# Windowed attention with a mixture of experts: blocks taken by position over all batches, and expert weights as float32 halves on the loads' own queue

## The chip, the cores and the metric

The kernel runs on one core of one Trainium2 chip. The metric is the device time of one execution in microseconds (us). A core has five engines with an instruction stream each: PE (TensorE, matrix products; its weight loads are shown apart as PEld), DVE (VectorE), ACT (ScalarE), POOL (GpSimd) and SP (SyncE, which here only issues DMA transfers). They run side by side and wait for each other by semaphores. Data in main memory comes into SBUF, the on-chip memory of 128 partitions, by DMA; PE writes its results to PSUM.

## The reference

Sliding-window attention with sink keys, then a mixture of four experts over all tokens. The sizes are B, H, S, D = 4, 8, 768, 64; 4 sink keys, a window of 128; 3072 tokens of 512 values, four experts with a hidden layer of 1024.

```python
scores = scale * np.matmul(q, k.transpose(0, 1, 3, 2))
keep = is_sink | in_window            # pos < 4, or 0 <= query - key < 128
scores = np.where(keep, scores, -1000000000.0)
a = softmax(scores)                   # written out in the reference
attn_out = np.matmul(a, v)
x = attn_out.transpose(0, 2, 1, 3).reshape(B * S, H * D)
p = domain_probs / (domain_probs.sum(-1, keepdims=True) + 1e-09)
for e in range(E):
    h = np.maximum(x @ w1[e], 0.0)
    out += p[:, e:e + 1] * (h @ w2[e])
```

Inputs and output are float32. A block of 128 queries needs its own 128 keys, the 128 keys before them, and, from the third block of a batch on, the four sink keys, which then lie outside its window.

## The kernel before

**Units.** The attention is cut into 24 blocks of 128 queries, numbered u = 0 to 23. `divmod(u, NQB)` gives the batch b and the position qb in it: batch 0's six blocks come first, then batch 1's. A block's way is: `load` q, k, v (256 KB each, float32, by SP); `cast` to bfloat16 on POOL; transposes of q and k (`pe_tr` on PE for u < 8, where u = 0 and 1 are transposed in float32 without a cast; `dma_q`, `dma_k` on SP's queue after that); `scores` (L340) into PSUM, against one key block where qb is 0 and two otherwise; `maxima` on DVE (L352: scale, mask and row maximum in one operation per head); `exps` on ACT (L360); transposes of the attention weights (`pe_a` and `a_out` for u < 8, `dma_a` after that); `values` (L420); `sums` and `normalise` on DVE; and a transpose into `xT` (`pe_x` or `dma_x`), which the experts read.

**Sinks.** Blocks with qb >= 2 have scores with the sink keys (`sink_scores`, `sink_minima`, `sink_args`, `sink_exps`). Their part of the result is made in two ways: for u < 8 (UPS) by one more matmul in `values` with a block-diagonal tile `vsd` (L417), and for u >= 8 by `weigh_sinks` on POOL, four products and three sums of 128x512 (L186, L190) that read `vsb`, the batch's sink values spread over all partitions by a transfer of 1 MB. `normalise` adds them (L449).

**Keys.** `kT` holds a batch's transposed keys in six slots, one for each position; two batches are held at a time.

**Experts.** An item is 512 tokens (four blocks) and one expert; the first 512 tokens with expert 0 are four items of 128. `mm1` (L495) makes the hidden layer from `w1[e]` and `xT`, `relu` moves it to SBUF, `mm2` (L521) makes 128 tokens of the output from `w2[e]`, and `collect` adds it, times the token's share, into `out_sb`, which `store` writes out. With `LATE`, the last expert of the first 512 tokens comes after three experts of the next 512. The last group's second layer is `last_group` (L537, L541).

**Weights.** `load_w1` and `load_w2` fetch a whole matrix of an expert (2 MB of float32) by a DMA of POOL's queue that casts to bfloat16 as it goes. The eight are issued after chosen casts of v (`w_after`).

**Order.** Nothing is scheduled on the chip. A planner in the kernel, at build time, keeps a table `nodes` with each step's engines and assumed costs, the steps that it needs, and a due time `want`; it takes the step that can start first, with the earliest due time among equals, and records it. So every engine has one fixed order, and an instruction that waits holds all behind it on its engine. `MOVED` shifts due times by hand. Loads are chained in the order of the list `loads`; the planner's model of the DMA queues (`transfers`, `SHARED`) tells it when data will be there. Until the first `mm2`, `keep_busy` puts matmuls without a use (idle_out, L482) where it sees PE idle.

Of the kernel before, what the change touches and what calls it, by code (L numbers as in the profile page):

```python
# [16 lines left out]
def kernel(  # L17
# [43 lines left out]
    UPS = 8  # L61

    UG = 4

    UF = 2

# [11 lines left out]

    NBS = -(-(UPS - 2) // NQB)
    vs = resid.tile([HS, B, D], FP32, name="vs", tag="vs")  # L80
    vsd = [resid.tile([P, H, D], BF16, name=f"vsd{b}", tag=f"vsd{b}") for b in range(NBS)]
# [3 lines left out]
    dp_nat = consts.tile([NTB, P, E], FP32, name="dp_nat")  # L85
# [7 lines left out]
    skd = [resid.tile([P, NHP, 2, NSINK], BF16, name=f"skd{i}", tag=f"skd{i}") for i in range(2)]  # L93
# [19 lines left out]
    M1 = consts.tile([P, 2, P], FP32, name="M1")  # L113
    M0 = consts.tile([P, P], FP32, name="M0")
    masks = [M0, M1, M2]

# [18 lines left out]
    for m in (M1, M2):  # L135
        nc.vector.memset(m, 0.0)
        own_keys(m[:, 1])
        keys_before(m[:, 0])
    nc.vector.memset(M1[:, 0, 0:NSINK], 0.0)


    bd = consts.tile([HS, H], FP32, name="bd")

    def sink_consts(eng):
        for t in Abuf:
            nc.gpsimd.memset(t[:, 2 * H], 0.0)
        for t in vsd:
            nc.gpsimd.memset(t, 0.0)
# [5 lines left out]
    def sink_heads(eng):  # L154
        nc.vector.reduce_sum(
            out=bd, in_=ident[0:HS, 0:HS].rearrange("p (h r) -> p h r", r=NSINK), axis=AX.X
        )

    def sink_values(eng, b):
        nc.gpsimd.tensor_mul(  # L160
            vsd[b][0:HS], vs[:, b, :][:, None, :].to_broadcast([HS, H, D]),
            bd[:, :, None].to_broadcast([HS, H, D]),
        )

# [3 lines left out]
    def spread_values(eng, b):  # L168
        vsb[b] = at_sb.tile([P, H, NSINK, D], FP32, name="vsb", tag="vsb", bufs=1)
        nc.sync.dma_start(  # L170
            out=vsb[b].rearrange("p h r d -> p h (r d)"),
            in_=v[b, :, 0:NSINK, :].rearrange("h r d -> h (r d)")[None].to_broadcast(
                [P, H, NSINK * D]
            ),
        )

    def sinks_on_pool(u):
        return u >= UPS and u % NQB >= 2

    def weigh_sinks(eng, u):  # L180
# [3 lines left out]
        for r in range(NSINK):  # L184
            t = sv if r == 0 else at_sb.tile([P, H, D], FP32, name="svr", tag="svr", bufs=1)
            nc.gpsimd.tensor_mul(  # L186
                t, vsb[u // NQB][:, :, r], pr[:, :, r : r + 1].to_broadcast([P, H, D])
# [17 lines left out]
    kT = {}  # L205
# [4 lines left out]
    def load(eng, u, what):  # L210
        b, qb = divmod(u, NQB)
# [6 lines left out]
    def cast(eng, u, what):  # L218
        t = raw.pop((what, u))
        if what == "v":  # L220
            vn[u] = resid.tile([P, H, D], BF16, name="vn", tag="vn", bufs=5)
# [15 lines left out]

    def load_sinks(eng):
        for h in range(H):
            nc.sync.dma_start(  # L240
                out=vs[h * NSINK : (h + 1) * NSINK],
                in_=v[:, h, 0:NSINK, :].rearrange("b r d -> r b d"),
            )
# [18 lines left out]
    def keys_of(b):  # L262
        if b not in kT:
            kT[b] = at_sb.tile([P, NHP, NQB, P], BF16, name="kT", tag="kT", bufs=2)
        return kT[b]
# [9 lines left out]
    def dma_k(eng, u):  # L275
        b, qb = divmod(u, NQB)
        nc.sync.dma_start_transpose(
            out=keys_of(b)[:, :, qb],
            in_=nat.pop(("k", u)).rearrange("p h d -> p (h d)"),
        )  # L280
# [13 lines left out]
    def k_out(eng, u):  # L294
        b, qb = divmod(u, NQB)
        copy_on(eng, keys_of(b)[:, :, qb], live.pop(("trk", u)))

    def sink_keys(eng, b):
        for c in range(2):
            r = slice(c * D, (c + 1) * D)  # L300
            copy_on(eng, skd[b % 2][r, :, c], kT[b][r, :, 0, 0:NSINK])
# [735 lines left out]
```

## Time and profile before

Three runs took 395.13, 395.74 and 397.17 us, a median of 395.74. The profiled execution has a span of 395.2 us from its first instruction to its last.

| | busy us | share of the span | instructions |
|---|---|---|---|
| PE | 384.8 | 97% | 2513 |
| PEld | 194.8 | 49% | 2555 |
| DVE | 203.6 | 52% | 672 |
| ACT | 225.6 | 57% | 632 |
| POOL | 147.7 | 37% | 177 |
| span | 395.2 | | |
| TensorE clock granted | 1.000 | | |
| DMA, SP's queue (q1) | 43.09 MB | 51.2% of 16 engines | |
| DMA, POOL's queue (q0) | 8.39 MB | 13.1% of 16 engines | |

How to read it: an engine's busy time is the sum of its instructions. PE's contains matmuls that wait for data within the array and those without a use, so 97% is not yet 97% of useful work. "q1" is the queue that SP fills, "q0" the one that POOL fills; the bytes of q0 are counted after the cast to bfloat16. The share of a DMA queue is the time that its packets took, over 16 DMA engines and the whole span. In the chain of work that ended last, PE has 86% of the span and DMA 11%, most of it in transfers of k and v.

The column of a line group that says "idle before" is the time in which the engine stood idle just ahead of these instructions; behind the arrow is what ended it. In a timeline, the first number is the start, the second how long the entry lasted, and "x4" how many instructions are merged in it.

### The profile page before, as it was taken

Reading aid. Unit: us, or ns where it says so; the run is one execution under the profiler, and the core shown is the slowest. Engines: PE = TensorE matmul, PEld = TensorE weight load, DVE = VectorE, ACT = ScalarE, POOL = GpSimd, SP = SyncE. Lnnn points to the kernel's source line nnn. Section 1 sums busy time; section 2 is a strip of 40 time slices with the busy share of each in tenths; the row PEclk is TensorE's granted clock in tenths of the full one; section 3 lists DMA queues with packets and bytes.
Section 4 is the critical chain, followed back from the end, with each engine's and each line's share of the span. In section 5 each row is a group of like instructions: output and inputs, shape, how many; then the busy total and the mean of one; then the engine's idle time right before and its main releaser. Section 6 shows DMA issues by size and latency. Waiting matters only on the chain.

```text
span 395.2 us, 7309 instructions
## 1 busy us (share of the span) xinstructions
PE 384.8 (97%) x2513; PEld 194.8 (49%) x2555; DVE 203.6 (52%) x672; ACT 225.6 (57%) x632; POOL 147.7 (37%) x177
## 2 busy tenths in 40 slices
PE   8999999999999999999999999999999999999996
PEld 6777555544444444444444444444444444444443
DVE  3996787259364853843866734456455332200233
ACT  5896787666573663764754746466377333354320
POOL 3515050309928561074495740154943800000000
PEclk9999999999999999999999999999999999999999
DMA  8998999918599689986555996762751300200002
GB/s 188 204 203 166 190 200 194 243 40 165 129 148 219 131 194 255 209 195 93 114 111 123 200 226 138 159 140 62 199 120 21 48 13 2 80 28 1 0 2 107
DMA packets 148154, 51.95 MB, mean 131 GB/s; under 512 B 135548, under 2 KB 143100, under 8 KB 148116
## 3 DMA queue, kind: packets, MB, share of 16 engines
q1 hardware_dynamic: 141844, 43.09, 51.2%
q0 software_dynamic: 6272, 8.39, 13.1%
q8 instruction: 20, 0.33, 0.3%
q14 instruction: 18, 0.15, 0.1%
HBM read 38.88 MB, written 6.29 MB: 114 GB/s over the span
## 4 chain that ended last, share of the span: by engine, by line
PE 86%; DMA 11%; issue 1%; POOL 1%; SPq 0%; DVE 0%; POOLq 0%
PE mopsum L521 40%; PE hpsum L495 39%; DMA rawk<-in_k_dram 5%; DMA rawv<-in_v_dram 5%; PE sp L340 3%; PE op L420 2%; DMA rawq<-in_q_dram 1%; PE lpsum L537 0%; PE tra L400 0%; PE trk L286 0%; PE trq L286 0%; PE ss L306 0%; POOL vn L200 0%; PE trx L471 0%; PE idle_out L482 0%
## 5 line engine op out<-in xcount | busy, mean ns | idle before, releaser
L495 PE MATMUL hpsum<-xT,w 128*128 128x512 bf16 (+1 forms) x843 | 182.5, 355 | 1.1
L521 PE MATMUL mopsum<-w,ht 128*128 128x512 bf16 x739 | 175.7, 379 | 1.6 <-issue 0.6
L509 ACT ACTIVATE ht<-hpsum 128x512 bf16<-128x512 f32 x172 | 102.0, 594 | 113.6 <-PE hpsum L495 100.8
L521 PEld LDWEIGHTS <-ht 128*128 128x128 bf16 x760 | 72.9, 98 | 87.7 <-issue 2.7
L495 PEld LDWEIGHTS <-w 128*128 128x128 bf16 x864 | 76.4, 98 | 79.0 <-issue 2.0
L562 DVE SCALAR_TENSOR_TENSOR out_sb<-mopsum,shares,out_sb 128x512 f32<-128x512 f32 x71 | 52.9, 746 | 109.2 <-PE mopsum L521 107.0
L360 ACT ACTIVATE A<-SM,negm 128x256 bf16<-128x256 f32 (+1 forms) x192 | 92.0, 481 | 16.6 <-DVE negm L352 13.6
L352 DVE CUSTOM_DVE_ANT_0 SM<-sp,M,slow 128x256 f32<-128x256 f32 x128 | 54.7, 479 | 8.6 <-PE sp L340 8.4
L190 POOL TENSOR_TENSOR sv<-sv,svr 128x512 f32<-128x512 f32 x36 | 45.6, 1267 | 2.8
L186 POOL TENSOR_TENSOR svr<-vsb,A 128x512 f32<-128x512 f32 x36 | 38.1, 1059 | 1.9
L200 POOL CAST qn<-rawq 128x512 bf16<-128x512 f32 x22 | 13.9, 634 | 62.1 <-DMA rawq<-in_q_dram 60.7
L360 ACT ACTIVATION_READ_ACCUMULATOR A<-SM,negm 128x1 f32 x192 | 36.3, 189 | 0.0
L186 POOL TENSOR_TENSOR sv<-vsb,A 128x512 f32<-128x512 f32 x12 | 13.0, 1082 | 62.5 <-ACT A L374 62.5
L558 ACT ACTIVATE out_sb<-mopsum,shares 128x512 f32<-128x512 f32 x19 | 13.0, 687 | 19.1 <-PE mopsum L521 19.0
L352 DVE CUSTOM_DVE_ANT_0 SM<-sp,M 128x128 f32<-128x128 f32 (+1 forms) x64 | 19.1, 351 | 5.9 <-PE sp L340 5.9
L200 POOL CAST kn<-rawk 128x512 bf16<-128x512 f32 x22 | 13.5, 614 | 19.7 <-DMA rawk<-in_k_dram 19.6
L200 POOL CAST vn<-rawv 128x512 bf16<-128x512 f32 x24 | 15.2, 633 | 12.5 <-DMA rawv<-in_v_dram 12.5
L449 DVE TENSOR_TENSOR both<-op,sv 128x512 f32<-128x512 f32 x12 | 8.3, 688 | 17.4 <-PE op L420 9.6
L340 PE MATMUL sp<-kT,qT 64*128 64x256 bf16 (+1 forms) x192 | 16.8, 271 | 0.0
L352 DVE DVE_READ_ACCUMULATOR2_ANT negm<- 128x1 f32 x192 | 15.9, 83 | 0.0
L420 PEld LDWEIGHTS <-AT 128*128 128x128 bf16 x352 | 13.4, 98 | 4.8 <-issue 0.2
L451 DVE TENSOR_TENSOR xn<-op,rs 128x512 bf16<-128x512 f32 x12 | 8.3, 688 | 14.5 <-PE op L420 14.1
(76 smaller groups left out, 197.5 us busy)
## 6 DMA issues: line engine op xcount, KB each, us to landing
w<-in_moe_w_dram POOLq DMA_DIRECT2D x8, 1024.0 KB, 12.8
rawq<-in_q_dram SPq DMA_DIRECT2D x24, 256.0 KB
rawk<-in_k_dram SPq DMA_DIRECT2D x24, 256.0 KB
rawv<-in_v_dram SPq DMA_DIRECT2D x24, 256.0 KB
out_dram<-out_sb SPq DMA_DIRECT2D x23, 256.0 KB
vsb<-in_v_dram SPq DMA_DIRECT2D x3, 1024.0 KB
AT<-A SPq DMA_TRANSPOSE x32
qT<-qn SPq DMA_TRANSPOSE x16
```

What stands on the lines that cost most here:

```text
L186: nc.gpsimd.tensor_mul(t, vsb[u // NQB][:, :, r], pr[:, :, r : r + 1].to_broadcast([P, H, D]))
L190: nc.gpsimd.tensor_add(sv, sv, t)
L200: nc.gpsimd.tensor_copy(out=out, in_=in_)
L340: nc.tensor.matmul(sp[h % 2][:, h // 2 % 2, lo:2], lhsT=qTb[u % 2][r, h // 2], rhs=kT[b][r, h // 2, qb - 1 + lo : qb + 1], start=True, sto ...
L352: nc.vector.tensor_tensor_reduce(out=SM[:, h][part], in0=live.pop(("sp", u, h))[part], in1=masks[min(qb, 2)], scale=-scale, scalar=live["s ...
L360: nc.scalar.activation(out=Abuf[u % 2][:, 2 * h + lo : 2 * h + 2, :], in_=SM[:, h, lo:2], func=AF.Exp, scale=-1.0, bias=live["negm", u][:, ...
L420: nc.tensor.matmul(op[:, h], lhsT=at[:, 2 * h + i], rhs=vn[u - 1 + i][:, h, :], start=(not sinks and i == lo), stop=(i == 1 and (h == H - ...
L495: nc.tensor.matmul(ps[:, j * n : (j + 1) * n], lhsT=w1[e][:, db, fb * P : (fb + 1) * P], rhs=xT[t0 // 512][:, db, t0 % 512 : t0 % 512 + n] ...
L509: nc.scalar.activation(out=ht, in_=ps, func=AF.Relu)
L521: nc.tensor.matmul(ps, lhsT=hidden(i, fb, sub), rhs=w2[e][:, fb, :], start=(fb == 0), stop=(fb == NFB - 1),)
L558: nc.scalar.activation(out=dst, in_=ps, func=AF.Copy, scale=sc)
L562: nc.vector.scalar_tensor_tensor(out=dst, in0=ps, scalar=sc, in1=dst, op0=ALU.mult, op1=ALU.add)
```

## The change

1. **Order of blocks.** `place(u)` replaces `divmod(u, NQB)`: u runs over the batches first, so that u = 0 to 3 are the first blocks of the four batches, u = 4 to 7 the second ones, and u >= 8 all those with sinks. `tile_of(u)` gives the block's place in the output, which `collect`, `last_group` and `store` now use. A block's neighbour before it is u - 4.
2. **Keys.** Each batch has its own `kT` with two slots, taken in turn by position (`qb % 2`); the mask that fits the swap is `M3`. Three of the masks are now made on POOL, as steps of the plan. Each batch has its own `skd`.
3. **Sinks.** The `vsd` path is gone with its tiles, its loads of `vs` and its matmul. Every block with sinks goes through `weigh_sinks`, and `vsb` is fetched for every such block, 16 times in place of 3.
4. **Weights.** Each matrix comes in two halves of 1 MB float32, by SP's queue, at places in the one list `loads` (`w_at`), into a ring `big` of three buffers that `vsb` shares; POOL or DVE then casts each half in two pieces. `mm1` waits for the half that it reads, `mm2` for both.
5. **Plan.** `LATE` is off: the four experts of the first 512 tokens come first. `starts`, `want_x` and `MOVED` have other numbers, and the DMA model is one queue in order.

```diff
+    NVN = 6
+    NBIG = 3
+    def place(u):
+        qb, b = divmod(u, B)
+        return b, qb
+    def tile_of(u):
+        b, qb = place(u)
+        return b * NQB + qb
...
-    skd = [resid.tile([P, NHP, 2, NSINK], BF16, name=f"skd{i}", tag=f"skd{i}") for i in range(2)]
+    skd = [resid.tile([P, NHP, 2, NSINK], BF16, name=f"skd{b}", tag=f"skd{b}") for b in range(B)]
+    kT = [resid.tile([P, NHP, 2, P], BF16, name=f"kT{b}", tag=f"kT{b}") for b in range(B)]
...
+    def later_mask(eng, m, own):
+        nc.gpsimd.memset(m, 0.0)
+        own_keys(m[:, own])
+        keys_before(m[:, 1 - own])
+        if m is M1:
+            nc.gpsimd.memset(m[:, 0, 0:NSINK], 0.0)
...
+    def big(name):
+        return at_sb.tile([P, 2048], FP32, name=name, tag="big", bufs=NBIG)
+    def spread_values(eng, u):
+        b, qb = place(u)
+        t = big("vsb")
         nc.sync.dma_start(
...
-    def load_w1(eng, e):
-        nc.gpsimd.dma_start(out=w1[e], in_=moe_w1[e].rearrange("(db p) f -> p db f", p=P))
-    def load_w2(eng, e):
-        nc.gpsimd.dma_start(out=w2[e], in_=moe_w2[e].rearrange("(fb p) d -> p fb d", p=P))
+    def half_of(e, layer, i):
+        if layer == 1:
+            fs = slice(i * (F // 2), (i + 1) * (F // 2))
+            return w1[e][:, :, fs], moe_w1[e].rearrange("(db p) f -> p db f", p=P)[:, :, fs]
+        bs = slice(i * (NFB // 2), (i + 1) * (NFB // 2))
+        return w2[e][:, bs], moe_w2[e].rearrange("(fb p) d -> p fb d", p=P)[:, bs]
+    def load_w(eng, e, layer, i):
+        t = big("wraw").rearrange("p (a c) -> p a c", a=4)
+        nc.sync.dma_start(out=t, in_=half_of(e, layer, i)[1])
+        wraw[e, layer, i] = t
+    def cast_w(eng, e, layer, i, j):
+        copy_on(
+            eng, half_of(e, layer, i)[0][:, 2 * j : 2 * j + 2],
+            wraw[e, layer, i][:, 2 * j : 2 * j + 2],
+        )
...
-        sinks = qb >= 2 and not sinks_on_pool(u)
-        if sinks:
-            nc.tensor.matmul(op, lhsT=at[:, 2 * H], rhs=vsd[b], start=True, stop=False)
         for h in range(H):
-            for i in range(lo, 2):
+            for i in blocks:
                 nc.tensor.matmul(
...
+                    op[:, h], lhsT=at[:, 2 * h + i],
+                    rhs=vn[u if i == own else u - B][:, h, :],
+                    start=(i == 0), stop=(i == blocks[-1]),
...
-        if sinks_on_pool(u):
-            both = at_sb.tile([P, H, D], FP32, name="both", tag="both", bufs=1)
-            nc.vector.tensor_add(both, res, live.pop(("sv", u)))
+        if u // B >= 2:
+            both = live.pop(("sv", u))
+            nc.vector.tensor_add(both, res, both)
...
-    LATE = True
+    LATE = False
...
-    w_after = [(2, "v"), (3, "v"), (4, "v"), (5, "v"), (6, "v"), (7, "v"), (10, "v"), (11, "v")]
+    w_at = [(1, 'v'), (2, 'v'), (3, 'k'), (3, 'k'), (3, 'v'), (3, 'v'), (5, 'q'), (5, 'q'), (5, 'k'), (5, 'k'), (5, 'v'), (5, 'v'), (6, 'k'), (7, 'k'), (8, 'k'), (9, 'q')]
+    halves_of_w = [(e, layer, i) for e in range(E) for layer in (1, 2) for i in range(2)]
+    for n, (e, layer, i) in enumerate(halves_of_w):
+        deps = [(("wc",) + halves_of_w[n - NBIG] + (j,), HOP) for j in range(2)] if n >= NBIG else []
+        node(("wl", e, layer, i), {"SP": 0.1}, lambda eng, e=e, l=layer, i=i: load_w(eng, e, l, i),
+             deps, -50.0, dma=2.7)
+        for j in range(2):
+            node(("wc", e, layer, i, j), {"POOL": 1.25, "DVE": 0.65},
+                 lambda eng, e=e, l=layer, i=i, j=j: cast_w(eng, e, l, i, j),
+                 [(("wl", e, layer, i), HOP)], -50.0)
...
+    for u in range(2 * B, NU):
+        if u - NBIG >= 2 * B:
+            deps = [(("sv", u - NBIG), HOP)]
+        else:
+            deps = [(("wc",) + halves_of_w[u - 2 * B - NBIG] + (j,), HOP) for j in range(2)]
+        node(("vsb", u), {"SP": 0.6}, lambda eng, u=u: spread_values(eng, u), deps,
+             nodes["load", u, "v"]["want"] + 0.1, dma=3.0)
...
         for g in range(NG):
+            have_w = [(("wc", e, 1, 2 * g // NG, j), HOP) for j in range(2)]
```

More of the change, by code (lines that the diff above doesn't have):

```diff
@@ L204 @@
     vn = {}
-    kT = {}
     xT = {}
@@ L385, in dma_a @@
         lo = half * H
-        hi = H if half == 0 else 2 * H + (1 if u % NQB >= 2 and not sinks_on_pool(u) else 0)
+        hi = lo + H
         nc.sync.dma_start_transpose(
@@ L832 @@
             d["want"] += MOVED.get(f"i{key[1]}", 0.0) + MOVED.get(key[0], 0.0)
-        elif len(key) > 1 and key[0] not in ("w1", "w2", "load", "sk", "vsd", "vsb"):
-            if key[1] < 9:
+        elif len(key) > 1 and key[0] not in ("wl", "wc", "load", "sk", "vsb", "mask"):
+            if key[1] < 16:
                 for name in (f"u{key[1]}", key[0], f"{key[0]}{key[1]}"):
```

301 lines of the change are left out of this document (124 added, 177 removed), and 4 rows, old and new, of the table MOVED.

## The prediction

> **What bounds the kernel now.** First the stages (busy time of each engine by stretch of the span):
>
> ```profile
> core 0: us, PE busy (x) PEld busy (x) DVE busy (x) ACT busy (x) POOL busy (x), PEclk, DMA share, GB/s
> 0.00:26.50 26.50, 23.33 (x246) 17.68 (x247) 18.75 (x93) 21.14 (x72) 10.60 (x27) 1.00 1.00 197
> 26.50:46.20 19.70, 19.43 (x262) 14.68 (x262) 14.38 (x53) 14.26 (x45) 5.28 (x8) 1.00 1.00 180
> 46.20:80.00 33.80, 32.62 (x261) 17.75 (x265) 20.57 (x79) 25.68 (x78) 8.85 (x14) 1.00 1.06 208
> 80.00:150.00 70.00, 69.47 (x413) 32.44 (x419) 42.26 (x134) 40.91 (x121) 42.69 (x44) 1.00 0.78 150
> ```
>
> From 80 us on PE has 0.5 us idle in 70: the rest of the span is PE's own work and nothing but less PE work shortens it. What can be won lies ahead, where DMA's share is 1.00. Then the timeline of PE there:
>
> ```profile
> 25.12 0.34 PE L482 MATMUL idle_out<-idle_in 128*128 128x128 bf16 x3
> ...
> 26.46 1.06 PE L495 MATMUL hpsum<-xT,w 128*128 128x128 bf16 x16
> ...
> 46.18 3.73 PE L495 MATMUL hpsum<-xT,w 128*128 128x512 bf16 x15
> ...
> 52.58 0.40 PE L286 MATMUL trk<-ident,kn 128*128 128x128 bf16 x4 [0.91 <-POOL kn L200]
> ```
>
> Until 26.46 us PE fills its time with dummies (idle_out); the first expert matmul starts there. The chain and POOL say what it waits for: loads of the attention inputs, while weights use the same DMA engines.
>
> ```profile
> 19.16 14.53 DMA rawv<-in_v_dram
> 34.98 16.78 DMA rawk<-in_k_dram
> ```
>
> ```profile
> 46.20 0.61 POOL L200 CAST qn<-rawq 128x512 bf16<-128x512 f32 x1 [7.62 <-DMA rawq<-in_q_dram]
> 51.91 0.61 POOL L200 CAST kn<-rawk 128x512 bf16<-128x512 f32 x1 [5.09 <-DMA rawk<-in_k_dram]
> ```
>
> A 256 KB load that lands 0.9 us behind its neighbour early on (POOL's casts at 11.11, 12.05 and 12.96 us) takes 14 to 17 us when a weight is under way.
>
> **PE's work, counted.** From the starts of neighbours on PE's timeline: four 512-column L495 matmuls 0.863 us, eight L521 1.73, sixteen 128-column L495 0.90, four float32 transposes 0.88, four bf16 transposes 0.22, a block's scores 0.55 (0.28 with one key block), values 0.46 (0.23), sink scores 0.11, a vsd matmul (L417) 0.21. Over all instructions of before: experts 332, attention 39.5, together 371.4. Of it 11.0 stands ahead of the matmul at 26.46, so PE is 15.5 us behind its work there; e=1's second layer starts at 58.81 with 41.4 ahead of it, 17.4 behind; the last matmul ends at 391.5, 20.1 behind. So 17.4 is lost by 59 us, 2.7 in the 333 us after it, and 3.7 behind the last matmul (span 395.2).
>
> **The change part by part.**
>
> PE work. The four vsd matmuls (L417, 0.9 us) go and 20 of the 116 transposes of L400 (1.1 us: no sink columns, and four early blocks with one key block in place of two); the rest is the same work in another order. After: 369.4, that is -2.0.
>
> Loads. Nothing changes until v of u=1, whose cast starts at 9.61. From there the DMA order is a single line, so landings add up: 0.95 us for each q, k, v load (the POOL casts above) and h for a float32 half of 1 MB. No row shows that transfer. Lower bound: its rows are 2 KB, and packets of 2048 bytes (stores of out_sb) take 84 ns in the packet records, 512 x 84 / 16 = 2.69 us. Upper bound: the old weight queue,
>
> ```profile
> q0 software_dynamic: 6272, 8.39, 13.1%
> ```
>
> 13.1% of 395.2 is 51.8 us for eight matrices of 2 MB float32, 3.24 us for each MB. I take 2.85: the busiest microsecond of the stores starts 187 packets (2.74), and the old queue shared its engines with other packets. Eight tiny vs loads also leave SP (12.90 to 17.88, 5 us in which q of u=4 waited); SP's issue of a load, 0.4 to 1.5 us, stays under the transfer.
>
> Casts of weights: 32 of 128x1024, half of them on POOL and half on DVE in the built order. POOL's 128x512 casts take 0.61, so 1.22 each; DVE's price is bounded by 0.42 (its bf16 PSUM copies, per 512) and 0.69 (its float32 PSUM casts), 0.84 to 1.38. Beside POOL's 1.22 a half is ready 1.2 to 1.4 us after landing; I use 1.2. POOL idles in waits for loads over most of the first 60 us (15.9 busy of 46.2), which hides its 20 us; DVE has 13 us free in the third stage, and about 6 us less to do in u=0 to 3 (32 maxima 0.21 apart, where 8 stood 0.21 and 24 stood 0.35 to 0.41 apart, and no sink work), for casts of 13 to 22 us in all, spread over 80. Without that cover each cast would add its 1.2 us to every gate below. The mask work on POOL (six selects of 0.29, three memsets of 0.2 to 0.5) fits before 9.6, where POOL idles 2.15 and 2.30 us.
>
> Gates. For each wait: landing, plus cast, less the PE work ahead of it, is how far PE is behind.
> - w2 of e=0, second half (4 halves, 5 loads after 9.6): 25.75 + 1.2 - 14.5 = 12.5. The work ahead is the attention of u=0 to 2, the scores and transposes of u=3, and six first-layer groups of 0.90.
> - w1 of e=2, first half (9 halves, 11 loads): 45.7 + 1.2 - 33.4 = 13.5.
> - k of u=6 (12 halves, 14 loads): 57.1 + 0.6 - 44.1 = 13.6.
> - w1 of e=3, first half: 13 halves, 14 loads, 60.0 + 1.2 - 48.7 = 12.5; its second half 11.1.
> - w2 of e=3, second half: near 80, with 74.2 of work ahead: no gate.
>
> The latest is 13.6, and PE does not fall further behind by loads. ACT, nearly full in the first stage (21.14 of 26.5), is not later: 32 exps 0.385 us apart, with its copies and relus, end u=3's attention at 27.2, and its values stand behind one second-layer group (1.73) that starts at the first gate, 27.0.
>
> Later units. All 16 blocks u>=8 weigh their sinks on POOL, 12 before. From
>
> ```profile
> L190 POOL TENSOR_TENSOR sv<-sv,svr 128x512 f32<-128x512 f32 x36 | 45.6, 1267 | 2.8
> L186 POOL TENSOR_TENSOR svr<-vsb,A 128x512 f32<-128x512 f32 x36 | 38.1, 1059 | 1.9
> ```
>
> one costs 3 x 1.27 + 4 x 1.06 = 8.06, with three casts 9.9 us a block. vsb goes from 3 to 16 transfers of 1 MB; one alone (its packets at 233.7 to 238) takes 4.3 us. A block then has on the DMA queue: 4.3, loads 3 x 0.95, five transposes about 3.5 (half a microsecond per 128 KB at 1000 packets a microsecond), a store 0.7: 11.4 us. Between the scores of u=8 and u=15 PE has 84.3 us of work, 12.0 a block; from u=16 it has 14 to 15. SP issues them in line: the wait of vsb for sv of three blocks before holds the transposes behind it, whose casts stand behind the same sv on POOL anyway. So this is covered, by 0.6 us a block; I cost it at nothing and keep both ends: 0, or what the third rival gives.
>
> Sum: 369.4 + 13.6 + 2.7 + 3.7 = 389.4 against a span of 395.2, -5.8. The median of runs stands 0.5 above that span: 389.9, so about 390.
>
> The Trainium skill ("SBUF — State Buffer", Who interferes with whom) speaks against the DVE casts: an SBUF-to-SBUF float32 copy on DVE takes a port pair shared with GpSimd, and one of the two blocks fully. No run here shows it: DVE's copies all read PSUM. By that rule a half's two casts come one after the other, which the second rival prices.
>
> **Rivals.**
> 1. The weight stays as slow as on its old queue (3.24). Then k of u=6 lands at 61.8, 18.3 behind, 394.1 in the span: no change. For it: the same HBM bytes by the same engines. Against: the 256-byte packets that ran beside them then (0.6 to 1.5 thousand per matrix).
> 2. POOL and DVE hold each other up when they cast at once. A half is ready at 1.2 + 0.8 to 1.4; that adds about 1 us to the gates and delays POOL's q and k casts by as much: 390.5 to 391.5. For it: nothing here; it is a rule of the page named above.
> 3. Slower: in u=8 to 15 the single queue is the bound. A block has 11.4 us of transfers in a fixed order, and SP waits in it. If a block takes more than PE's 12.0, PE, whose order is fixed too, stands at each scores: 7 intervals. At 13.1 us a block the gain is gone (7.8 us) and it is slower from there; at 13.5, 389.4 + 10.5 = 400. For it: 95% use of a queue with waits; before had 14.5 us of PE work a block there (101.4 between the same scores). Against: POOL waits 62.5 us for ACT before its sv, so blocks were not held by POOL or loads; and all 16 vsb need not fall in these eight blocks.
> 4. The change is not what it says: the built SP order shows the weights among the loads, so I give it nothing.
>
> **Numbers.** A difference of 0.5% (2 us) is what this measurement tells from none. Forecast 0.55, own range 387.5 to 392.5 (h 2.69 gives 388.5 on the runs' scale, 2.95 gives 391). First rival or anything between, 393 to 396: 0.17. Second: 0.10. Third: 0.18, of which 0.03 ends level. Faster 0.55 + 0.10 + 0.05 of the first = 0.70; level 0.12 + 0.03 = 0.15; slower 0.15. The range reaches from 387 to 397.
>
> **What would show it.** First expert matmul before 20 us, first L521 matmul (second layer) at 27 us, e=2's first layer at 47; no DMA wait of POOL over 5 us in the first 60. A landing interval near 2.85 us for halves. POOL near 193 us busy. It is wrong if PE's idle time after 80 us is above 4 us (third rival), or if PE waits for wraw casts by DVE that began over 1 us after landing (second).

## The result, and the profile after

The kernel before took 396.27 us in the runs beside it, the changed one 416.41 us (415.92 to 417.53): 1.051 times as long, interval 1.048 to 1.055. Forecast was 390. The profiled execution spans 414.2 us. First the stretches of the prediction, for the changed kernel:

```profile
core 0: us, PE busy (x) PEld busy (x) DVE busy (x) ACT busy (x) POOL busy (x), PEclk, DMA share, GB/s
0.00:26.50 26.50, 23.20 (x257) 19.25 (x257) 15.46 (x78) 18.04 (x69) 11.58 (x31) 1.00 1.04 251
26.50:46.20 19.70, 18.49 (x170) 11.36 (x169) 11.87 (x47) 12.75 (x41) 10.14 (x10) 1.00 1.02 311
46.20:80.00 33.80, 32.66 (x257) 17.28 (x261) 24.41 (x76) 25.12 (x71) 16.71 (x17) 1.00 1.06 302
80.00:150.00 70.00, 66.14 (x427) 31.52 (x433) 48.49 (x155) 39.95 (x123) 44.49 (x45) 1.00 1.06 220
150.00:210.00 60.00, 53.40 (x313) 24.56 (x317) 31.77 (x93) 27.93 (x81) 39.73 (x41) 0.94 1.11 209
210.00:414.20 204.20, 195.64 (x1077) 90.71 (x1096) 94.55 (x255) 91.02 (x235) 76.57 (x74) 1.00 0.55 113
```

Before, PE had 0.5 us idle from 80 to 150; now it has 3.9, 6.6 in the next 60 us, and 8.6 in the last stretch, of which 3.9 lie behind its last matmul. The DMA share from 80 to 150 is 1.06 (before 0.78), and it stays above 1.00 to 210. Moved bytes on the page of the changed kernel:

```profile
q1 hardware_dynamic: 163652, 73.47, 81.1%
HBM read 52.48 MB, written 6.29 MB: 142 GB/s over the span
```

q1 had 43.09 MB and 51.2%. Of the 30.4 MB more, 16.8 are the float32 halves, which POOL's queue carried before, and 13.6 are 13 more vsb. Next PE's, POOL's and SP's timelines around the longest wait (start, duration, and in brackets the idle time ahead and what ended it; SPq is SP issuing transfers):

```profile
179.81 0.81 PE L493 MATMUL hpsum<-xT,w 128*128 128x512 bf16 x3
185.78 0.27 PE L308 MATMUL ss<-skd,qT 128*128 128x8 bf16 x4 [5.16 <-DMA qT<-qn]
185.91 1.87 PE L493 MATMUL hpsum<-xT,w 128*128 128x512 bf16 x4
```

```profile
176.15 0.61 POOL L198 CAST qn<-rawq 128x512 bf16<-128x512 f32 x1 [3.14 <-DMA rawq<-in_q_dram]
```

```profile
170.92 1.46 SPq L389 DMA_TRANSPOSE AT<-A  x1
172.43 0.57 SPq L210 DMA_DIRECT2D rawq<-in_q_dram  x1
...
174.72 0.90 SPq L170 DMA_DIRECT2D vsb<-in_v_dram  x1
175.72 1.64 SPq L569 DMA_DIRECT2D out_dram<-out_sb  x1
177.47 3.93 SPq L275 DMA_TRANSPOSE qT<-qn  x1
```

This is block 15. SP issues its load of q at 172.43, in its fixed order right behind the AT transpose of block 13, that is 13.4 us before PE needs the result. POOL waits 3.14 us for q and casts it at 176.15; SP, behind 1 MB of vsb and a store, takes 3.93 us to issue q's transpose. PE, which has done all that its order allows, stands until 185.78. The four matmuls after it take 1.87 us where four take 1.03 elsewhere.

In the last stretch a wait of DVE has grown. Here are its line in DVE's view of waits (us in total, times, longest; all of it lies behind 200 us, where the kernel before has one such wait of 0.6) and two lines of PE's, for the whole span:

```profile
DVE sv L447 <- POOL sv L188: 29.8, 8, 7.6
```

```profile
PE ss L308 <- DMA qT<-qn: 7.8, 4, 5.2
PE mopsum L519 <- DVE out_sb L562: 2.5, 3, 1.3
```

DVE stands at L447 for POOL's sv, and the sums of the experts (L562) wait behind it in DVE's order; PE gets no free PSUM buffer.

**Where the time went.** As in the prediction, "behind" is the start of an instruction on PE less the work built ahead of it. The changed kernel's scores of u = 8 start at 93.8 with 72.0 of work ahead, 21.8 behind; those of u = 16 at 213.9 with 179.5, 34.4 behind; its last matmul ends at 410.3, 40.9 behind 369.4. The table has the same three numbers for every kernel of this study, from its profiled execution, beside the median of its runs and its ratio to the kernel before with the interval.

| kernel | behind at u = 8 | more to u = 16 | more to the end | span | runs | ratio |
|---|---|---|---|---|---|---|
| before | 17.7 | 0.9 | 1.5 | 395.2 | 396 | |
| changed | 21.8 | 12.6 | 6.5 | 414.2 | 416.4 | 1.048 to 1.055 |
| vsb4 | 22.0 | 6.0 | 5.6 | 406.6 | 407.7 | 1.025 to 1.037 |
| late_vsb | 22.1 | 16.7 | 5.6 | 417.7 | 419.5 | 1.054 to 1.065 |
| sv1 | 21.8 | 14.9 | 4.5 | 414.4 | 416.8 | 1.049 to 1.056 |
| keep_bf16 | 25.2 | 6.1 | 5.6 | 410.8 | 411.3 | 1.036 to 1.042 |
| hoist | 24.9 | 9.5 | 5.5 | 413.3 | 414.1 | 1.042 to 1.048 |
| hoist_vsb4 | 26.3 | 2.2 | 5.5 | 407.0 | 407.0 | 1.026 to 1.032 |
| w_on_pool | 25.5 | 11.8 | 5.7 | 416.6 | 417.8 | 1.051 to 1.058 |
| ring4 | 24.0 | 10.3 | 5.9 | 413.1 | 417.4 | 1.049 to 1.057 |
| true_costs | 22.2 | 0.9 | 25.2 | 421.0 | 422.4 | 1.063 to 1.070 |
| true_ahead3 | 23.2 | 16.8 | 6.3 | 419.1 | 418.9 | 1.052 to 1.062 |
| keep_true | 23.6 | 2.7 | 2.0 | 401.6 | 402.8 | 1.012 to 1.026 |
| halves_alone | 25.0 | 1.4 | 2.0 | 403.0 | 404.3 | 1.017 to 1.027 |
| no_casts | 20.9 | 11.0 | 7.2 | 412.5 | 415.3 | 1.043 to 1.055 |
| no_loads | 17.8 | 13.3 | 11.7 | 416.3 | 412.7 | 1.037 to 1.044 |
| casts_on_pool | 21.2 | 12.0 | 5.8 | 411.7 | 416.2 | 1.044 to 1.053 |
| order_alone | 26.8 | 1.5 | 1.8 | 403.0 | 406.0 | 1.020 to 1.028 |
| before_vsb12 | 18.6 | 3.0 | 10.7 | 407.3 | 403.1 | 1.018 to 1.023 |
| keep_late | 24.5 | 2.2 | 2.0 | 402.3 | 403.6 | 1.019 to 1.023 |

The profiles of no_loads and before_vsb12 are of executions slower than those kernels' other runs, so neither their last column of "behind" nor a single wait in them is read. The early column moves by up to 3 us between kernels that are alike there (vsb4 22.0, hoist 24.9), which the last section explains in part; a difference of that size in it shows nothing.

### The profile page after: what moved, and what is told of

It reads as the page before. It is cut to its first block, busy times and chain, and to the rows that moved or that the text cites. A ratio compares the mean times of both kernels' runs of the same rounds, so it can differ in the third digit from the quotient of the medians.

```text
span 414.2 us, 7318 instructions
## 1 busy us (share of the span) xinstructions
PE 389.5 (94%) x2491; PEld 194.7 (47%) x2533; DVE 226.5 (55%) x701; ACT 214.8 (52%) x615; POOL 199.2 (48%) x217
## 3 DMA queue, kind: packets, MB, share of 16 engines
HBM read 52.48 MB, written 6.29 MB: 142 GB/s over the span
## 5 line engine op out<-in xcount | busy, mean ns | idle before, releaser
L519 PE MATMUL mopsum<-w,ht 128*128 128x512 bf16 x746 | 173.9, 379 | 3.3 <-DVE out_sb L562 2.5
L507 ACT ACTIVATE ht<-hpsum 128x512 bf16<-128x512 f32 x162 | 95.0, 593 | 112.3 <-PE hpsum L493 60.9
L519 PEld LDWEIGHTS <-ht 128*128 128x128 bf16 x760 | 73.4, 98 | 89.6 <-issue 4.8
L562 DVE SCALAR_TENSOR_TENSOR out_sb<-mopsum,shares,out_sb 128x512 f32<-128x512 f32 x71 | 52.6, 744 | 70.4 <-PE mopsum L519 66.1
L188 POOL TENSOR_TENSOR sv<-sv,svr 128x512 f32<-128x512 f32 x48 | 61.2, 1275 | 3.8
L184 POOL TENSOR_TENSOR svr<-vsb,A 128x512 f32<-128x512 f32 x48 | 50.8, 1058 | 2.5
L184 POOL TENSOR_TENSOR sv<-vsb,A 128x512 f32<-128x512 f32 x16 | 17.6, 1103 | 58.5 <-ACT A L376 58.4
L198 POOL CAST w<-wraw 128x1024 bf16<-128x1024 f32 x16 | 24.5, 1531 | 35.1 <-DMA wraw<-in_moe_w_dram 35.1
L505 DVE TENSOR_SCALAR ht<-hpsum 128x512 bf16<-128x512 f32 x30 | 20.5, 685 | 14.2 <-PE mopsum L519 11.7
L447 DVE TENSOR_TENSOR sv<-op,sv 128x512 f32<-128x512 f32 x16 | 11.0, 688 | 30.2 <-POOL sv L188 29.8
L198 POOL CAST vn<-rawv 128x512 bf16<-128x512 f32 x24 | 15.8, 657 | 14.4 <-DMA rawv<-in_v_dram 12.7
L558 ACT ACTIVATE out_sb<-mopsum,shares 128x512 f32<-128x512 f32 x17 | 11.6, 684 | 21.2 <-PE mopsum L519 21.2
L317 DVE TENSOR_SCALAR sneg<-ss 128x32 f32<-128x32 f32 x16 | 3.0, 187 | 26.3 <-PE ss L308 26.3
L196 DVE CAST w<-wraw 128x1024 bf16<-128x1024 f32 x16 | 11.1, 691 | 11.5 <-DMA wraw<-in_moe_w_dram 11.3
```

Source lines behind the costliest of these rows:

```text
L184: nc.gpsimd.tensor_mul(t, vsb[u][:, :, r], pr[:, :, r : r + 1].to_broadcast([P, H, D]))
L188: nc.gpsimd.tensor_add(sv, sv, t)
L198: nc.gpsimd.tensor_copy(out=out, in_=in_)
L505: nc.vector.tensor_scalar_max(out=ht, in0=ps, scalar1=0.0)
L507: nc.scalar.activation(out=ht, in_=ps, func=AF.Relu)
L519: nc.tensor.matmul(ps, lhsT=hidden(i, fb, sub), rhs=w2[e][:, fb, :], start=(fb == 0), stop=(fb == NFB - 1),)
```

## The experiments

**What fills u = 8 to 15.** Three runs: fewer vsb transfers, their place in the line, and POOL's sv.

```diff
     def spread_values(eng, u):                      # vsb4
+        if u >= 12:
+            vsb[u] = vsb[9 + u % 3]
+            return
...
     def spread_values(eng, u):                      # late_vsb
+        later[u] = 1         # issued in dma_k(u), behind its transpose
...
-        for r in range(NSINK):                      # sv1
+        for r in range(1):
```

> The changed kernel with 12 of its 16 vsb transfers left out, plan and order of every engine as they are; from u = 12 on POOL weighs with the sink values of another batch, so that part of the result is not computed. If the 12 MB on SP's one queue hold PE up: PE has 369.4 us of work, is 21.8 behind it at u = 8 as before this cut, loses about 2.4 more to the last matmul, 3.9 behind it: a span near 397.5, 399 to 400 as a run; no PE wait for qT or AT above 1 us in u = 9 to 15. If POOL's sv (8 us a block) is what holds the blocks: 414 to 416, as the changed kernel. If the transfers only share the blame with the plan, something between, 404 to 410.

> The changed kernel with all 16 vsb transfers, each issued right behind the k transpose of its block in place of ahead of it; all other orders are kept. If the place in the line matters (1 MB directly ahead of the transposes that PE needs): PE no longer waits 5 us at u = 15 and 8 to 12 of the 12.6 us that it loses between u = 8 and u = 16 come back: 404 to 408. If bytes matter alone (the queue is full whatever the order): 413 to 417. If sv now gets its values late, DVE's wait for sv grows and the time with it: above 417.

> The changed kernel with all 16 vsb transfers, but POOL weighs one sink key in place of four (one product of 1.1 us a block in place of 8.06; three keys are left out of the result). If the queue holds PE up: 411 to 417, with the 5 us wait at u = 15 still there (only DVE's waits for sv, 2 to 3 us in all from u = 16 on, go). If POOL's chain holds the blocks: 396 to 402.

With 4 of 16 transfers the loss between u = 8 and u = 16 halves, 12.6 to 6.0, and the runs fall by 8.7 us. The four that stay are those of u = 8 to 11. From u = 12 on, where vsb4 has none, it loses 0.8 us to u = 16 and the changed kernel 9.3. Without seven eighths of POOL's sv they don't fall at all: a wait of 3.76 us for qT stands at the same block.

```profile
188.43 0.27 PE L308 MATMUL ss<-skd,qT 128*128 128x8 bf16 x4 [3.76 <-DMA qT<-qn]
```

So POOL's sv does not bound this stage, and the transfers are what costs time in it. A later place in the line was no help: the waits moved from qT to AT (PE's longest 6.85 us, ended by AT) and it got slower. If the transfers were all, vsb4 was to take 399 to 400; 6.0 us in the middle, 1.7 of them at half clock (133.1 to 136.6 us), and 5.6 behind it stayed.

**The chain of loads.** In vsb4 the rest of the loss stood between u = 10 and u = 12, in waits for qT and kT. So the loads of q and k were issued one place earlier, with 16 transfers and with 4.

```diff
     def dma_k(eng, u):                              # hoist, hoist_vsb4
         ...
+        for w in "qk":
+            if u + 1 < NU and (w, u + 1) not in raw and ("q", u + 1) not in nat:
+                load(eng, u + 1, w)
+                early.add((w, u + 1))
```

> The changed kernel with all 16 vsb transfers; only the loads of q and k of block u + 1 are issued one place earlier on SP, right behind the k transpose of block u, in place of behind the AT transposes of block u - 1 (where they wait for ACT's exps). Two theories of the 12.6 us lost between u = 8 and u = 16: (a) a chain, loads issued late, then 1 MB of vsb, cast, transposes, scores, exps, AT, next loads, which takes 13.4 us a block: then 6 to 11 us come back, 405 to 410, and PE's waits for qT go; (b) the queue has no room for 11.4 us of transfers in 12 us: then at most 2 us come back, 414 to 417, and the waits for qT turn into waits for AT or kT.

> The earlier q and k loads with 12 of the 16 vsb transfers left out too (sink values of other batches from u = 12 on, so that part is not computed). The run with 4 transfers lost 6.0 us between u = 8 and u = 16, all of it between u = 10 and u = 12 in waits for qT and kT. If those are late loads: lag about 22.5 at u = 16 in place of 28.0, and 401 to 403. If the rest has another cause (the four vsb transfers in a row, two halves of a weight among them): 406 to 408, as with the 4 transfers alone.

Earlier loads alone take 3.1 us off the middle (9.5): the wait of 5 us for qT goes, one of 2.9 for xT comes; fewer transfers alone take 6.6 off; together 10.4, and only 2.2 remain. By its time, hoist (414.1) is where a queue without room was expected (414 to 417); with 4 transfers the earlier loads take 3.8 off the middle, as was expected of a chain. Both theories hold a part: a block is a chain of transfers (load, vsb, cast, transpose, scores, exps, AT, next load), and each MB of vsb lies on it. The runs show none of the 3.8: hoist_vsb4 was to take 401 to 403 if late loads were the rest, and its median is no better than that of vsb4. In its profiled execution the early stage came out 4.3 us later.

**Sink values kept.** They are only four different MB; in bfloat16 two of them fit in one buffer of the ring.

```diff
     def spread_values(eng, u):                      # keep_bf16
+        if qb > 2:
+            vsb[u] = vsb[u - B]
+            return
+        if b % 2 == 0:
+            pair[0] = at_sb.tile([P, 2, 2048], BF16, name="vsb", tag="big", bufs=NBIG)
-        nc.sync.dma_start(
+        nc.gpsimd.dma_start(
```

> The changed kernel with the sink values of the four batches fetched once each, as bfloat16 by POOL's queue, and kept in two of the ring's three buffers (they fit: 4 KB each a partition); result complete. If the queue's bytes are the cause: as the run with 4 transfers, 397 to 401. If POOL's issue of the four transfers or their slower queue costs something: one delay of 2 to 4 us near u = 8, 400 to 404. If POOL's sv is the bound: 414 to 416.

The middle is that of vsb4 (6.1), with the result complete; but 397 to 401 were expected if bytes were the cause, and the 411.3 us have 3.4 us more in the early stage and 5.6 at the end.

**The plan.** It assumed 3.0 us for vsb, 7.3 for sv and so on.

```diff
-{"POOL": 7.3}                   # sv
+{"POOL": 8.2}
-dma=3.0)                        # vsb
+dma=4.3)
-{"POOL": 1.25, "DVE": 0.65}     # casts of weights
+{"POOL": 1.56, "DVE": 0.7}
-    AHEAD = 2
+    AHEAD = 3                   # true_ahead3 alone
```

> The changed kernel, result complete, with the durations that its own profile shows put into its plan in place of the assumed ones: vsb 4.3 us on the queue (3.0), loads 1.2 (1.1), sv 8.2 on POOL (7.3), casts of weights 1.56 and 0.70 (1.25 and 0.65); the plan orders all engines anew. If the loss from u = 8 on is mostly a bad order (DVE's sums of the experts held behind a wait for sv, transposes behind vsb): 402 to 408. If the chain of one block's loads behind the AT transposes of two blocks before is the limit whatever the order: 413 to 418.

> As the run with true costs, and the loads of block u need only the AT transposes of u - 3 to be issued, not those of u - 2 (AHEAD 3). If the chain load, vsb, cast, transpose, scores, exps, AT, next load is the limit: 8 to 14 us faster than the run with true costs and 400 to 406. If the queue's bytes are: within 3 us of it.

> True costs, AHEAD 2, and the sink values fetched once for each batch (4 transfers, bfloat16, POOL's queue) with the plan made for it; result complete. With the chain shorter by the 1 MB and DVE's order right: lag 22 to 25 at u = 8 as before, 1 to 3 us more to u = 16, 2 to 3 more to the end: 396 to 401. If the early stage alone (21.8 behind at u = 8 against 17.7) keeps it above the kernel before, it ends at 397 or more; if under 395, the queue's bytes and the order were everything.

Truer costs with 16 transfers made it slower, 422.4: attention now keeps pace to u = 16 (0.9 lost), then falls behind: PE waits 8.4 us for one xT and 4.8 for one AT, and its clock is at half from 287.6 to 304.8. Loads issued a block sooner made it 3.5 us faster, where 8 to 14 were expected if the chain were the limit (418.9, with 16.8 in the middle). With the sink values fetched once for each batch, 4 transfers, and a plan made for it with the same costs, it is at 402.8 us, which was to be 396 to 401. Two of its stretches, PE's largest wait, and its bytes:

```profile
80.00:150.00 70.00, 67.90 (x458) 32.62 (x457) 46.74 (x146) 43.69 (x129) 45.41 (x46) 1.00 0.97 170
150.00:210.00 60.00, 58.85 (x362) 27.29 (x361) 42.24 (x123) 33.02 (x99) 43.65 (x46) 1.00 0.69 143
```

```profile
PE ss L314 <- DMA qT<-qn: 2.1, 2, 1.8
```

```profile
HBM read 39.90 MB, written 6.29 MB: 115 GB/s over the span
```

12.6 MB less are read (52.48 to 39.90), POOL is as busy as in the changed kernel (199.7 and 199.2 us), and the two late losses fall from 12.6 and 6.5 to 2.7 and 2.0, the last only where plan and transfers were both mended (keep_bf16 had 5.6). Against the kernel before, 2.3 us of the loss from u = 8 on remain.

**The transfers in the old order.** Here a block has 14.5 us of PE work.

```diff
-        if u % NQB == 2 and ("vsb", u // NQB) in nodes:
-            loads.append(("vsb", u // NQB))
+        if ("vsb", u) in nodes:
+            loads.append(("vsb", u))
```

> The kernel before with the sink values fetched for every block that POOL weighs, 12 transfers of 1 MB in place of 3, two buffers, planned anew; all else as before; result complete. If it is the pace that decides (11.4 us of transfers in PE's 12.0 us of work a block, against 14.5 here): the queue has room and it stays within 3 us: 395 to 399. If a 1 MB transfer ahead of the transposes stretches the chain of waits in any order: 403 to 412.

9 MB more, with a second buffer for vsb and a plan made anew, cost 7.7 us there too (403.1, where 395 to 399 were expected if the pace of the blocks decides). So the transfers cost without the shorter block as well: a queue with room on paper is no cover for 1 MB in the chain. How much of it is the new plan's, and at which wait it is lost, this run does not show.

**The early stage.** Five runs ask why PE is 21.8 behind at u = 8.

```diff
-        nc.sync.dma_start(out=t, in_=half_of(e, layer, i)[1])                       # w_on_pool; cast_w does nothing
+        nc.gpsimd.dma_start(out=half_of(e, layer, i)[0], in_=half_of(e, layer, i)[1])
...
-        t = big("wraw")...                                                          # ring4
+        t = spare[0] if n in (3, 7, 11) else big("wraw")...
...
     def cast_w(eng, e, layer, i, j):                                                # no_casts; no_loads: load_w too
+        if e:
+            return
...
         copy_on(                                                                    # casts_on_pool
-            eng, half_of(e, layer, i)[0][:, 2 * j : 2 * j + 2],
+            "POOL", half_of(e, layer, i)[0][:, 2 * j : 2 * j + 2],
```

> The changed kernel with its weights on POOL's DMA queue, cast to bfloat16 by the DMA as before, each half issued at the place in the plan where SP would issue it; no casts on POOL and DVE; all else as it is. It tells whether the new way of the weights or the new order of blocks costs the first 94 us (PE is 21.8 us behind its work at u = 8; before 17.7). If the single queue and the casts cost them: lag 16 to 18 at u = 8, 410 to 412. If the new order of blocks does: 21 to 23, 415 to 418. If the order of landings was worth what the prediction thought and only shared: lag above 24, 419 to 423.

> The changed kernel with a fourth buffer for weights (three halves, the 4th, 8th and 12th, go to the output buffer of the second 512 tokens, idle until then), so a half no longer waits for the casts of the third half ahead of it. In the changed kernel three halves were issued just when such a cast ended (27.55, 46.20 and 52.87 us). If the ring holds the early loads up: lag at u = 8 down by 2 to 4 us from 21.8, and 412 to 414. If the queue is full anyway: lag within 1 us of 21.8, 415 to 417.

> The changed kernel with the 12 halves of experts 1 to 3 still transferred but not cast: 24 casts on POOL and DVE are left out, and all experts compute with the weights of expert 0 (the products of experts 1 to 3 are not the reference's). Plan and order as they are. If the casts (26 us of POOL and DVE time, DVE's copies ahead of maxima, a buffer that comes free late) make the early gates: lag at u = 8 down from 21.8 to 18 or less, 410 to 413. If the transfers make them: 20.5 to 22, 414 to 417.

> As no_casts, and the 12 transfers are left out too (12 MB less). If the queue is what makes the early stage late: lag at u = 4 down from 17.9 to 16 or 17 (its gate is of expert 0), and no growth from there to u = 8 (17 to 18 in place of 21.8): 411 to 413, and 3 to 5 us under no_casts. If PE's early lag comes from the attention's own chain of DVE, ACT and POOL: as no_casts, within 1.5 us.

> The changed kernel with the 16 casts that DVE does moved to POOL at the same places of the plan. In the changed kernel a cast of 128x1024 takes POOL 1.04 us where DVE stands still and 1.56 beside DVE's cast of 0.69. If two engines hold each other up: 1.04 each for all 32, so a half is ready 2.1 us after landing (1.6 now), DVE has 11 us less, and the time stays within 2 us of 416; all at 1.5 or more would mean that something else slows them, and 418 to 421.

On the old queue the weights put PE 23.4 behind at u = 3 (14.9 in the changed kernel) and 25.5 at u = 8: in these two profiles the halves look like a gain early, but the runs show only 1.4 us of it, less than can be measured. A fourth buffer and casts on POOL alone changed nothing measurable. In the other four kernels PE is 17.4 to 18.7 behind at u = 4 (17.9 in the changed kernel). From there to u = 8 the changed kernel loses 3.9 more, no_casts 2.2, and no_loads 0.4. So in these profiles the 12 halves behind the first four cost 3.5 us there, and the runs of no_loads agree (412.7, 3.7 us under the changed kernel). Of the 3.5, 1.7 go with the casts and 1.8 with the transfers, too little to call one of them the cause. The other 17.4 are there with four halves and the first loads alone.

**One part at a time.**

```diff
-        nc.gpsimd.dma_start(out=w1[e], in_=moe_w1[e].rearrange(...))     # halves_alone, on the kernel before;
+        nc.sync.dma_start(out=t, in_=half_of(e, layer, i)[1])            # order_alone the reverse, on keep_true
...
-    LATE = False                                                         # keep_late, on keep_true
+    LATE = True
```

> The kernel before in its own order of blocks, with only its weights changed: float32 halves on SP's queue, a ring of three buffers shared with vsb (3 transfers), cast in SBUF by POOL or DVE, the plan with the measured costs and the halves placed anew among the loads (dp_nat, both and two hidden tiles give the space). Result complete. In the changed kernel the weights on POOL's queue put PE 3.7 us further behind at u = 8. If the halves are worth that in either order: 391 to 394. If they only help where blocks come by position: 395 to 399. If the casts on DVE and the single line cost more than they bring: above 400.

> The new order of blocks by position, the sink values fetched once for each batch as in keep_true, and the weights as in the kernel before (whole matrices on POOL's queue, issued behind casts of v, no casts in SBUF), planned with the DMA model of before; result complete. PE's work is 369.4. If the halves are the loss of the early stage: lag near 17.7 at u = 8, 2 to 3 more to u = 16, 2 to the end: 394 to 397, level with the kernel before. If the order by position needs its data earlier than the old way gives them: lag 21 to 25, 398 to 404. If the order is a gain that the halves hid: under 394.

> As keep_true (blocks by position, sink values fetched once for each batch, halves on SP's queue), with the last expert of the first 512 tokens behind three experts of the next 512 (LATE, as before) and the plan made anew with loads at 1.3 us and halves at 3.0 on the queue, its due times and places of the halves chosen again; result complete. If the early loss is 12 MB asked of the queue too soon: lag at u = 8 between 18 and 21 (23.6 in keep_true) and 395 to 399, level with the kernel before at best. If the early lag comes from the order by position itself: 22 to 25 and 400 to 404.

None reaches the kernel before. Halves in the old order: 404.3, with 25.0 behind at u = 8, 3.2 of it in one wait for a sum of DVE. The new order with the old weights: 406.0, 26.8 behind, 3.9 of it in a wait for a weight of expert 3. Both together with the sink values kept: 402.8 to 403.6, with or without LATE. Each plan was made anew, so a few us of the early column are the plan's and not the part's; what is shown is that no part alone, and no pair without the 12 extra transfers, brought a gain with the one plan that each was given.

## Why the prediction was wrong

The sum was 369.4 + 13.6 + 2.7 + 3.7 = 389.4; measured is 369.4 + 21.8 + (12.6 + 6.5) + 3.9 = 414.2. So 8.2 us are missing in the gates and 16.4 in the term for all that comes after them.

- **PE work, -2.0.** The count bears it out (96 transposes of L400 in place of 116, no matmul of L417). No run tests the durations behind it, since "behind" is by definition the difference to them.
- **The step that failed first, "So this is covered, by 0.6 us a block; I cost it at nothing".** The prediction added up 11.4 us of transfers a block against 12.0 of work and took a sum under the line as no loss. The eight blocks took 13.4 us each in the mean (93.8 to 187.7 over seven intervals). vsb4, before_vsb12 and, against true_costs, keep_true show that the transfers cost this time, and sv1 that POOL's sv does not. Why 11.4 became 13.4 is shown in part. The queue did not stand idle (the last column is GB/s; the DMA share, a sum over packets, can pass 1.00):

```profile
93.80:187.70 93.90, 85.70 (x527) 39.78 (x536) 59.72 (x192) 52.03 (x160) 64.15 (x65) 0.98 1.10 215
...
111.00:112.00 1.00, 1.00 (x7) 0.41 (x6) 0.76 (x2) 1.00 (x4) 0.00 (x0) 1.00 1.11 414
...
114.00:115.00 1.00, 1.00 (x6) 0.42 (x5) 0.00 (x0) 0.73 (x2) 0.92 (x2) 1.00 0.29 26
```

  By the packet records, some packet is under way in all but 1.65 of these 93.9 us, while the transfers in them (6.7 vsb, 18 loads, 34 transposes, 8 stores) come to some 76 us at the prediction's prices (an estimate). But what was moved in a microsecond went from 414 GB/s to 26, with 215 in the mean. The price of a load was too low (1.2 us, see below). The other thing cost at nothing is the chain, which goes through SP: of the 93.9 us its issues take 84.0 (72.1 of 101.4 between the same scores before), a transpose no less than 1.21, and it waits 14.4 us for ACT ahead of AT and 7.1 for POOL ahead of qT. No run tells the queue's pace from SP's. And in the pause of 5.16 us the clock was halved, which made this wait 2.5 us dearer.
- **The term of 2.7 us for the end.** The prediction looked at POOL's sv only as cover for transposes. DVE waits for it too, and the sums of the experts stand behind that in DVE's order; 6.5 us were lost in place of 1.5 before. Directly shown are PE's 2.5 us of waits for out_sb; sv1, with no long sv, has none of them. In keep_true, planned with sv at 8.2 and 12 MB less, it is 2.0. POOL is not the whole of it: sv1 still lost 4.5, with a wait of 1.6 us for qT among it, vsb4, whose DVE waits as long for sv (30.3 us), 5.6, and keep_bf16, with few transfers and the plan of the change, also 5.6. What the rest is stays open.
- **Gates: the loads' price, 0.95 us.** POOL's casts of the first and the fourth half begin at

```profile
13.10 1.04 POOL L198 CAST w<-wraw 128x1024 bf16<-128x1024 f32 x1 [2.20 <-DMA wraw<-in_moe_w_dram]
...
30.36 1.56 POOL L198 CAST w<-wraw 128x1024 bf16<-128x1024 f32 x1 [2.83 <-DMA wraw<-in_moe_w_dram]
```

  where the fourth was to land at 25.75: 4.6 us late. From 8 to 60 us SP issued 12 halves and 14 loads and the queue moved 16.3 MB; at 2.85 and 0.95 that would be 47.5 us and it took 52, which leaves 1.27 for a load if a half has 2.85 (an estimate from these numbers). The profile tells the two prices apart. From 13 to 15 us, where only loads move, the queue moves 218 to 219 GB/s, 1.2 us for 256 KB; from 42 to 45, where only halves move, 375 GB/s, 2.8 us for 1 MB. So the half was priced rightly, and the first rival (3.24) is answered: the loads are dear, not the halves. The 0.95 came from the kernel before, which moved 240 to 264 GB/s from 10 to 13 us. Why it is 218 to 222 here, from 5 to 9 us already, before a packet of a half moves, is not shown. SP's issues of loads, priced at 1.5 us at most, took up to 4.06 in the first 80 us. With all this the gate of w2 of e = 0 is 16.7 behind (31.22 us, predicted 27 and 12.5). The gate of w1 of e = 0, second half, was not in the list at all; it stands at 22.50, 14.8 behind, which is already above the 13.6 that was to be the latest.
- **Second rival, DVE's and POOL's casts.** The mechanism is there: a cast of 128x1024 takes POOL 1.04 us alone and 1.53 in the mean beside DVE's. The group of POOL's casts in the changed kernel, then with all casts on POOL:

```profile
L198 POOL CAST w<-wraw 128x1024 bf16<-128x1024 f32 x16 | 24.5, 1531 | 35.1 <-DMA wraw<-in_moe_w_dram 35.1
```

```profile
L198 POOL CAST w<-wraw 128x1024 bf16<-128x1024 f32 x32 | 32.4, 1040 | 30.1 <-DMA wraw<-in_moe_w_dram 30.1
```

  The Trainium skill's rule ("SBUF — State Buffer", Who interferes with whom) agrees with these rows. Its price was 1 us a gate in the prediction; moving the casts changed the time by less than can be measured.
- **Third rival.** It came true in its place and its size, with 13.4 us a block where its 13.5 gave 400, but not in its form: PE does not stand at each scores. Of the 12.6 us, 2.5 fall between the scores of u = 10 and 11, 6.1 between 14 and 15, and 3.0 between 15 and 16. The other 14 us of the span are the gates (8.2) and what the middle and the end lost beyond its 10.5 and 2.7 (5.9). Its chance, 0.18, was too low: the argument against it (POOL waits 62.5 us for ACT before its sv) says that POOL was free, not that the queue was, and 6.7 of the 1 MB transfers did fall into its seven intervals.
- **What was to show it.** First expert matmul at 17.02, as said, and no DMA wait of POOL above 3.65 us in the first 60. But the first L519 matmul (then L521) is at 31.22 in place of 27, and e = 2's first layer at about 52 in place of 47. PE's idle time from 80 us to its last matmul is 3.9 + 6.6 + 4.7, above the 4 that the text named as the sign of the third rival. POOL is busy for 199.2 us, not 193; the casts of weights at 1.53 in place of 1.22 are 5 of the 6.

What stays open: of the early 21.8 us some 3.5 belong to the 12 halves behind the first four; the 17.4 at u = 4, where the kernel before has 15.6, are not split further between loads, four halves and the attention's own chain on ACT and DVE.

## What to carry to other kernels

A queue that serves several links of one block's chain can't be costed by adding its transfers and comparing the sum with the engine's work: 95% on paper was a loss of 12 us here. Take the prices from the mix in which the transfers will run, and count the time of the engine that issues them. Before data is fetched again because the bytes are "hidden", count how often it is the same data: 4 fetches in place of 16 were worth 5 us with the plan of the change (keep_bf16), and 20 between two kernels planned with measured costs (true_costs and keep_true). A plan with fixed orders carries its assumed durations into every wait; put measured ones in, but expect nothing of it while the true bound stays.

## What the runs showed of the hardware

**The clock halves without one long pause.** In the changed kernel PE stands 5.16 us and the granted clock is at 0.50 from about 184.1, 3.5 us into the pause, to 190.9 (windows of 1 us; PE busy first, granted clock third from the end):

```profile
183.00:184.00 1.00, 0.00 (x0) 0.00 (x0) 0.00 (x0) 0.00 (x0) 1.00 (x2) 1.00 0.34 48
184.00:185.00 1.00, 0.00 (x0) 0.00 (x0) 0.00 (x0) 0.00 (x0) 0.92 (x2) 0.56 0.07 23
185.00:186.00 1.00, 0.22 (x5) 0.22 (x6) 0.00 (x0) 0.00 (x0) 0.92 (x2) 0.50 1.30 253
...
190.00:191.00 1.00, 1.00 (x4) 0.38 (x3) 0.40 (x1) 0.51 (x3) 0.80 (x1) 0.53 1.23 278
191.00:192.00 1.00, 1.00 (x6) 0.45 (x5) 1.00 (x4) 0.27 (x1) 0.59 (x1) 1.00 1.25 216
```

Some 5 us at half speed cost 2.5 more. In hoist it happens at about 85.7 with no pause longer than 1.01 us (windows of 0.8 us):

```profile
82.00:82.80 0.80, 0.46 (x3) 0.10 (x1) 0.80 (x4) 0.29 (x1) 0.80 (x1) 1.00 1.10 339
82.80:83.60 0.80, 0.13 (x2) 0.10 (x1) 0.80 (x4) 0.46 (x3) 0.79 (x2) 1.00 1.15 338
83.60:84.40 0.80, 0.43 (x8) 0.30 (x7) 0.80 (x7) 0.80 (x4) 0.00 (x0) 1.00 1.24 270
84.40:85.20 0.80, 0.48 (x8) 0.31 (x6) 0.80 (x4) 0.80 (x5) 0.00 (x0) 1.00 1.05 271
85.20:86.00 0.80, 0.68 (x7) 0.44 (x6) 0.80 (x3) 0.80 (x4) 0.00 (x0) 0.81 1.09 374
86.00:86.80 0.80, 0.80 (x3) 0.30 (x2) 0.78 (x4) 0.48 (x1) 0.10 (x1) 0.50 1.02 384
```

PE was busy for 1.50 of 3.2 us there, in small transposes that waited for ACT and DVE, and then ran at half speed to about 89.1, 1.7 us lost. The changed kernel has shorter waits there (0.37 and 0.32 us) and keeps its clock. In all profiles of this study a half-speed stretch that ends before the kernel does lasts 3.41 us (hoist) or a multiple of it (6.83 here, 17.07 in true_costs), so a PE with work loses at least 1.7. Such stretches are a part of what moves the early column of the table: 1.7 of hoist's 3.1 more, and keep_true has one too (0.91 in the mean from 26.5 to 46.2). They need not come in each execution: the mean clock of hoist's four runs is 0.988 to 1.000. And they are not all: keep_late has none and is 24.5 behind. The Trainium skill ("TensorE: Matmul & The Clock Gate", Part 1: The HAM clock gate) has the halving after an idle window of about 3.4 us; the first case agrees with it, the second shows it for a window that was not idle but less than half busy.

**An issue can hold the issuing engine for microseconds.** SP's issue of a 128 KB transpose took 3.93 us behind 1 MB of vsb (177.47 above), where others took 1.21 to 1.27; all that SP was to issue next waited with it. That a full queue held it is inferred: no view shows the queue's length.

**1 MB is not 1 MB.** A vsb in packets of 1 KB took 4.3 us alone (233.7 to 238 in the kernel before), a half in packets of 2 KB 2.8 us (42 to 45 in the changed one).
